# Attention with thresholded softmax and routed experts on one core: value products gathered into every second slot

## The chip, the cores and the metric

The kernel runs on one core of one Trainium2 chip. The metric is device time in microseconds. Three runs of the kernel before gave 980.18 us in the median, 979.74 to 981.54.

## What is computed

Two layers in one launch. Attention over 8 batches, 8 heads, 576 tokens and head size 64, in which every score that lies more than tau below its row's maximum is dropped, and then a mixture of 8 experts in which tokens choose experts greedily under a capacity of 576:

```python
scores = scale * np.matmul(q, k.transpose(0, 1, 3, 2))
thresh = np.max(scores, axis=-1, keepdims=True) - tau
scores = np.where(scores >= thresh, scores, -1000000000.0)
...
attn = np.exp(scores)
attn = attn / (np.sum(attn, axis=-1, keepdims=True) + 1e-09)
return np.matmul(attn, v).astype(np.float32)
...
logits = x @ w_gate          # x: 4608 x 512, then greedy assignment, cap = 576
h = np.maximum(x[mask] @ w1[e], 0.0)
out[mask] = h @ w2[e]        # for each of the 8 experts
```

## The kernel before

Attention takes the first 455 us, the search that assigns tokens to experts starts right behind it, and the experts' matrix products fill the rest. The change touches attention and the stretch in which its last rows are written out; the code of the search and of the experts is the same in both kernels.

**Tiles.** Heads are taken two at a time: 4 head pairs in a batch, 32 in all. Two head pairs (c in the code) make 9 units of queries: four of 128 queries for each pair, and the fifth (u = 4) holds the last 64 queries of both. A unit of two heads is two tiles of 128 queries by 576 keys. A **slot** of the loop handles one unit's two tiles in every stage of the pipeline, so there are 144 slots, and two head pairs take 9 of them.

**Stages of a slot.** TensorE computes the scores (score, line 79) into a tile sc of two PSUM banks, of which the scores fill 288 of 512 columns in each; there are two such tiles, one for each of the slot's two tiles. VectorE takes the row extreme and a scaled copy z (mx, line 87). ScalarE computes the exponentials (ex, line 95) into pp. One slot later VectorE drops what is below the threshold and sums the rows (stt, line 98). Then TensorE transposes pp in blocks of 64 keys (turn, line 108): the first 8 of the 9 key blocks into one PSUM tile tb of which there is one only (tr), which ScalarE copies to pt (trev, line 123). The **ninth** key block of a unit goes into the free columns of a score tile (left), and ScalarE copies it out of there (leftev, lines 136 and 139). The value products of a head pair (group, line 151) run over 9 key blocks, accumulate in the PSUM tile vb, and are copied to xt when the ninth is in (shut, line 155). The trace records each float32 matmul as two, so a key block of products is 8 recorded matmuls; a transpose is recorded once.

**Order.** Each engine runs in the order in which the code issues. In a slot TensorE has: the scores of both tiles, the ninth blocks of one or two units (in 5 of 9 slots), a piece of value products, the 16 transposes of the unit. The dictionary plan gives the pieces: a head pair's 9 key blocks are spread over four slots as 3, 2, 2 and 2; 8 slots of 9 have a piece, and the remaining one has the gate's logits of a finished batch (lg_unit, line 174, or lgt_unit). The transposes' tile is copied out in the next slot. The ninth blocks sit in the score tile of the slot's second tile, and ScalarE copies them out between the two exponentials. For two batches finished rows are transposed into the free columns of score tiles too (rows_turn), at two slots of 9.

**End.** The products of the last two head pairs, the last logits, and then 18 late rows (late_unit, line 218): 8 transposes of 128 by 128 into tb or vb by turns, one copy by ScalarE (line 220), and a copy of 16 factors (line 222) for two units of three; then the rows are written to memory. The first steps of the search (a phase of the Router, whose counting matmuls are at line 453) are issued between the late rows by a small planner, with XTY us from one late row to the next.

Of the kernel before, what the change touches and what calls it, by code (L numbers as in the profile page):

```python
# [18 lines left out]
S=576; D=64; HS=288; QK=2*HS+2*S; NB=9; SL=3; XE=8*HS  # L19
PPB=8; LTB=1; VTB=4; HOLD=1; XW=520; NBO=2; NDEF=4; XTB=4; XTY=1.35; XT0=2.0; XRB=2  # L20


def attention(ctx, tc, qk, vl, tau, wgd, xrows, xts, Lg, nb_batches, ident, swap, R, after_first):
# [101 lines left out]
    def left(s_,t,only=None):  # L125
        c,u=divmod(s_,9)
        if u not in (1,3,6,8) and u!=only or s_<0: return
        sc=SC[t] if t is not None else ps_s.tile([128,2,512],F32,name="sc"); LB[s_]=sc
        for i,n in enumerate((u,) if u==4 else (u-1,u)):
            turn(sc[:,:,HS+64*i:HS+64*i+64],PB.pop((c,n)).rearrange("p k h d -> p k (h d)")[:,8])  # L130
    def leftev(s_):
        c,u=divmod(s_,9)
        if s_ not in LB: return
        sc=LB.pop(s_)
        if u==4:
            for a in range(2): A.activation(pt_of(2*c+a)[:,8].rearrange("p (f q) -> p f q",f=2)[:,:,0:32],sc[:,a,HS:HS+64].rearrange("p (f q) -> p f q",f=2),AF.Copy)
        else:
            p,g=tile_of(c,u); o=at(g-1)
            A.activation(pt_of(p)[:,8,o:o+256].rearrange("p (i r q) -> p r i q",i=2,r=2),sc[:,:,HS:HS+128].rearrange("p r (i q) -> p r i q",i=2),AF.Copy)
# [42 lines left out]
    def lgt_unit(b,ps):  # L182
        lt=LT[b]
        for c in range(5):
            o=at(c) if c<4 else S
            turn(ps[:,:,64*c:64*c+64],lt[:,o:o+128])
    def lv_of(ps): return ps[:,:,:320].rearrange("p r (c j x) -> p r c j x",c=5,j=2)[:,:,:,:,:16]
    def lgt_ev(b,ps):
# [26 lines left out]
    def late_unit(b,qb,k):  # L215
        ps=(ps_v.tile([128,2,512],F32,name="vb") if k%2 else ps_t.tile([128,2,512],F32,name="tb")).rearrange("p a b -> p (a b)")
# [57 lines left out]
    for s_ in range(-2,NT//2+2):  # L274
        st["slot"]=s_
        sc_=[t for t in (2*s_+4,2*s_+5) if 0<=t<NT]; tr_=[t for t in (2*s_,2*s_+1) if 0<=t<NT]
        tt_=[t for t in (2*s_+2,2*s_+3) if 0<=t<NT]; ev_=0<=s_-1<z; gate=None
        for t in sc_: score(t)
        if ev_: left(s_-1,sc_[-1] if sc_ else None)
        if (s_-5)%9==SL: left(s_-1-SL,sc_[-1] if sc_ else None,4)  # L280
        if s_==9: R.consts2()
# [31 lines left out]
        if 0<=s_<z: tr(s_)  # L313
# [648 lines left out]
```

## Time and profile before

| | |
|---|---|
| median of three runs | 980.18 us |
| the profiled execution | 980.79 us, span 979.1 us |
| TensorE matmul busy | 939.3 us, 96% |
| VectorE, ScalarE, GpSimd busy | 761.3, 620.2, 241.3 us |
| chain that ended last | TensorE 83%, ScalarE 6%, VectorE 5%, DMA 2% |
| attention's loop, first to last row extreme of slots 5 to 141 | 25.50 to 435.71 us |
| its last late row copied, search counting ends | 478.8 us, 481.6 us |

Times are from the span's start. The busy column of TensorE contains the modelled tail of each matmul, so a TensorE that is called 99% busy may still wait a little; how densely it works is read from the starts of its instructions. What ended an idle stretch stands behind an arrow.

### The profile page before, as it was taken

Reading aid. Unit: us, or ns where it says so; the run is one execution under the profiler, and the core shown is the slowest. Engines: PE = TensorE matmul, PEld = TensorE weight load, DVE = VectorE, ACT = ScalarE, POOL = GpSimd, SP = SyncE. Lnnn points to the kernel's source line nnn. Section 1 sums busy time; section 2 is a strip of 40 time slices with the busy share of each in tenths; the row PEclk is TensorE's granted clock in tenths of the full one; section 3 lists DMA queues with packets and bytes.
Section 4 is the critical chain, followed back from the end, with each engine's and each line's share of the span. In section 5 each row is a group of like instructions: output and inputs, shape, how many; then the busy total and the mean of one; then the engine's idle time right before and its main releaser. Section 6 shows DMA issues by size and latency. Waiting matters only on the chain.

```text
span 979.1 us, 25952 instructions
## 1 busy us (share of the span) xinstructions
PE 939.3 (96%) x10365; PEld 718.5 (73%) x10365; DVE 761.3 (78%) x2070; ACT 620.2 (63%) x1064; POOL 241.3 (25%) x334
## 2 busy tenths in 40 slices
PE   6999999999999999998789999999999999999996
PEld 4666666666666666665679798897988979898994
DVE  7999999999999999993679878587887786535220
ACT  6889989999899998984445354352452525445330
POOL 2222423333242423220020412222303123210202
PEclk9999999999999999999889999999999999999999
DMA  5213242431523141205651615243523435341101
GB/s 205 87 54 108 72 157 68 156 133 57 183 69 98 44 145 53 99 2 198 235 181 43 217 44 185 66 158 103 164 91 135 125 124 153 120 134 38 38 11 44
DMA packets 38936, 107.63 MB, mean 110 GB/s; under 512 B 7456, under 2 KB 8224, under 8 KB 38304
## 3 DMA queue, kind: packets, MB, share of 16 engines
q1 hardware_dynamic: 31424, 83.36, 25.1%
q0 software_dynamic: 5888, 19.03, 6.3%
q10 hardware_dynamic: 1504, 3.59, 1.2%
q8 instruction: 82, 1.34, 0.6%
q14 instruction: 38, 0.31, 0.1%
HBM read 83.51 MB, written 21.38 MB: 107 GB/s over the span
## 4 chain that ended last, share of the span: by engine, by line
PE 83%; ACT 6%; DVE 5%; issue 2%; DMA 2%; POOL 0%; POOLq 0%; ACTq 0%; SPq 0%; DVEq 0%
PE pf L800 21%; PE pf L832 20%; PE vb L151 13%; PE sc L79 12%; PE tb L108 8%; ACT pp L95 3%; PE pt L745 2%; DVE pp L98 1%; PE sc L108 1%; PE rps L453 1%; DVE z L87 1%; ACT pt L123 1%; ACT pt L120 1%; DMA out_dram<-y,idx 1%; PE vb L174 1%
## 5 line engine op out<-in xcount | busy, mean ns | idle before, releaser
L95 ACT ACTIVATE pp<-z,nb 128x576 f32<-128x576 f32 x288 | 218.4, 777 | 39.9 <-DVE z L87 39.1
L98 DVE SCALAR_TENSOR_TENSOR pp<-z,nb,pp 128x576 f32<-128x576 f32 x288 | 223.8, 814 | 0.0
L87 DVE TENSOR_SCALAR_CACHE_REDUCE z<-sc 128x576 f32<-128x576 f32 x288 | 206.6, 752 | 18.7 <-PE sc L79 11.8
L832 PE MATMUL pf<-w2h,H 128*128 128x512 f32 x576 | 194.3, 401 | 0.2 <-DVE H L381 0.2
L79 PE MATMUL sc<-qk 64*128 64x288 f32 (+1 forms) x1280 | 173.5, 419 | 3.1 <-DMA qk<-qk_dram 1.9
L88 POOL TENSOR_SCALAR nb<-nb,taub 128x2 f32<-128x2 f32 x144 | 99.0, 687 | 284.2 <-ACT pp L95 180.3
L151 PE MATMUL vb<-pt,vt 64*64 64x288 f32 x2232 | 164.9, 416 | 0.3 <-ACT pt L120 0.3
L123 ACT ACTIVATE pt<-tb 128x1024 f32<-128x1024 f32 x128 | 131.0, 1023 | 8.3 <-PE tb L108 7.8
L108 PEld LDWEIGHTS tb<-ident,pp 64*128 64x128 f32 x2304 | 83.5, 139 | 70.9 <-ACT pp L95 36.0
L832 PE MATMUL pf<-w2l,H 128*128 128x512 f32 x320 | 128.6, 402 | 0.0
L839 POOL DMA_INDIRECT out_dram<-y,idx x40 | 45.6, 1140 | 307.5 <-ACT y L835 270.4
L832 PEld LDWEIGHTS pf<-w2h,H 128*128 128x128 f32 x576 | 106.7, 189 | 19.5 <-DVE H L381 0.7
L79 PEld LDWEIGHTS sc<-qk 64*128 64x128 f32 (+1 forms) x1280 | 96.7, 178 | 23.8 <-DVE z L87 4.0
L108 PE MATMUL tb<-ident,pp 64*128 64x64 f32 x2304 | 103.1, 230 | 10.2 <-ACT pt L120 4.3
L151 PEld LDWEIGHTS vb<-pt,vt 64*64 64x64 f32 x2232 | 73.5, 133 | 50.7 <-issue 8.8
L800 PE MATMUL pf<-xh,w1h 128*128 128x288 f32 (+2 forms) x512 | 109.9, 301 | 0.7 <-ACT xh L746 0.7
L800 PE MATMUL pf<-xh,w1l 128*128 128x288 f32 (+2 forms) x512 | 110.4, 301 | 0.0
L800 PE MATMUL pf<-xl,w1h 128*128 128x288 f32 (+2 forms) x512 | 110.1, 301 | 0.0
L835 ACT ACTIVATE y<-pf 128x512 f32<-128x512 f32 x40 | 23.9, 597 | 124.6 <-PE pf L832 115.4
L812 ACT ACTIVATE hf<-pf 128x576 f32<-128x576 f32 x56 | 36.5, 651 | 90.4 <-PE pf L800 85.9
L800 PEld LDWEIGHTS pf<-xh,w1h 128*128 128x128 f32 x512 | 82.1, 190 | 1.6 <-ACT xh L746 1.1
L800 PEld LDWEIGHTS pf<-xl,w1h 128*128 128x128 f32 x512 | 82.0, 190 | 0.0
(189 smaller groups left out, 1202.9 us busy)
## 6 DMA issues: line engine op xcount, KB each, us to landing
qk<-qk_dram SPq DMA_DIRECT2D x31, 864.0 KB, 5.1
w2s<-w_dram SPq DMA_DIRECT2D x32, 512.0 KB, 4.4
w1s<-w_dram SPq DMA_DIRECT2D x28, 512.0 KB, 5.1
vt<-vl_dram SPq DMA_DIRECT2D x32, 288.0 KB, 4.3
xrows<-pp SPq DMA_DIRECT2D x24, 260.0 KB, 2.6
xts<-xt SPq DMA_DIRECT2D x2, 1152.0 KB, 5.2
pt<-xts SPq DMA_DIRECT2D x2, 1152.0 KB, 6.7
xrows<-xr SPq DMA_DIRECT2D x8, 260.0 KB, 2.6
```

What stands on the lines that cost most here:

```text
L79: T.matmul(sc[o,f,:HS], LD[p]["q",h][r,q], LD[p]["k",h][r,:],start=True,stop=True)
L87: V.tensor_scalar(z,SC.pop(t)[:,:,:HS],-0.125,None,op0=ALU.mult,op1=ALU.min,accum_out=nb[:,0,t%2:t%2+1])
L88: G.tensor_scalar(nb[:,1],nb[:,0],taub[:,0:1],None,op0=ALU.add)
L95: A.activation(pview(t),zview(t),AF.Exp,bias=NBI[t][:,0:1],scale=-1.0)
L98: V.scalar_tensor_tensor(pv,zview(t),NBI[t][:,1:2],pv,op0=ALU.is_le,op1=ALU.mult,accum_out=den_of(t//36)[:,n:n+1])
L108: g=slice(64*r,64*r+64); T.transpose(o[:,r],x[g],ident[g,g])
L123: A.activation(pt_of(p)[:,0:8,o:o+128].rearrange("p k (r q) -> p r k q",r=2),tb,AF.Copy)
L151: T.matmul(to[64*f:64*f+64,h,:HS],v[g,64*k:64*k+64],pt[g,k,HS*f:HS*f+HS],start=(k==0),stop=(k==8),skip_group_check=True)
L800: T.matmul(ps[:,h,:n],s[w][:,k,f*128:(f+1)*128],s[x][:,k,cols[h]],start=(i==0),stop=(i==11))
L812: A.activation(hf,ps[:,:,:HS],AF.Relu)
L832: T.matmul(ps[:,0,:],H[:,f,c:c+128],s[w][:,f],start=(f==0 and j==0),stop=e)
L839: G.indirect_dma_start(out=out,out_offset=IOA(ap=s["idx"][:n,t:t+1],axis=0),in_=y[:n],in_offset=None)
```

## The change

- The value products of a head pair stand in two slots instead of four, 4 key blocks and then 5, two slots apart. In a period of 18 slots the even slots but one have products, and the odd ones have none; slot 14 has the gate's logits and slot 15 their transposes.
- A unit's 16 transposes are issued one slot later, right behind the scores, and the products come last in a slot. The copy of the transposes follows in the same slot.
- The ninth blocks are issued between the scores of the slot's two tiles, into the first one's score tile, in 8 slots of 18, of which 7 are slots without value products; two units at a time, or three (with the unit of 64 queries). ScalarE copies them out ahead of the transposes' copy.
- Both exponentials of a slot are issued behind the transposes' copy.
- Rows of finished batches are transposed at three slots of 18 instead of two of 9, all in slots with products.
- At the end the next to last head pair's products are interleaved with the last units' transposes; the last logits' transposes are split, four columns of blocks and then the fifth; a late row is made with 16 transposes of 64 rows instead of 8 of 128, and its copy reads and writes contiguous columns; the planner's distance XTY is 1.25 instead of 1.35.

```diff
-    def mx(ts):
+    def mx(ts,between):
...
             z=wk.tile([128,2,HS],F32,name="z",bufs=5); ZB[t]=z
...
+            if t%2==0: between()
+        if ts: G.tensor_scalar(nb[:,1],nb[:,0],taub[:,0:1],None,op0=ALU.add)
+        else: between()
...
+    NINTH={3:0,7:1,9:2,11:3,13:4,16:5,17:6,1:7}
+    def left(s_,sc):
+        n=NINTH.get(s_%18)
...
+    def leftev():
+        if "now" not in LB: return
+        i0,sc=LB.pop("now"); c,u=divmod(i0,9); p,g=tile_of(c,u); o=at(g)
+        A.activation(pt_of(p)[:,8,o:o+256].rearrange("p (i r q) -> p r i q",i=2,r=2),sc[:,:,HS:HS+128].rearrange("p r (i q) -> p r i q",i=2),AF.Copy)
+        if u==2:
+            for a in range(2): A.activation(pt_of(2*c+a)[:,8].rearrange("p (f q) -> p f q",f=2)[:,:,0:32],sc[:,a,HS+128:HS+192].rearrange("p (f q) -> p f q",f=2),AF.Copy)
...
-        for i in range(8): T.transpose(ps[:n,128*i:128*i+128],xh(b)[:,i,o:o+n],ident)
+        for i in range(8): turn(ps[:n,:,64*i:64*i+64],xh(b)[:,i,o:o+n])
...
-    for p in range(NP-1):
-        n=0; o=9*(p//2)+(10 if p%2 else 6)
-        for i,m in enumerate((3,2,2,2) if p<NP-2 else (3,3,1)): plan[o+i-(p==NP-2)]=[(p,x) for x in range(n,n+m)]; n+=m
+    for p in range(NP-2):
+        o=18*(p//4)+(6,10,16,20)[p%4]
+        plan[o]=[(p,x) for x in range(4)]; plan[o+2]=[(p,x) for x in range(4,9)]
+    plan[z-2]=[(NP-2,x) for x in range(5)]
...
-        for t in sc_: score(t)
-        if ev_: left(s_-1,sc_[-1] if sc_ else None)
+        for t in sc_[:1]: score(t)
+        left(s_,SC[sc_[0]] if sc_ else None)
+        for t in sc_[1:]: score(t)
...
+        if 0<=s_-1<z: tr(s_-1)
...
+        mx(sc_,leftev)
...
+        if 0<=s_-1<z: turned(s_-1)
...
-        for t in sc_[1:]: ex(t)
+        for t in sc_: ex(t); SC.pop(t)
...
-        if 0<=s_<z: tr(s_)
         if s_==z-1:
+            for k in (5,6): group(NP-2,k)
+            tr(z-1); turned(z-1)
             for k in (7,8): group(NP-2,k)
...
-    lgt_unit(b,gp); lgt_ev(b,gp)
+    lgt_unit(b,gp,range(4)); w=lgt_ev(b,gp)
+    gp=ps_s.tile([128,2,512],F32,name="sc")
+    lgt_unit(b,gp,(4,)); lgm_ev(b,gp,w)
```

TensorE in the middle of the loop, before: scores are sc<-qk, ninth blocks sc<-ident,pp, products vb<-pt,vt, transposes tb<-ident,pp.

```order
L79 MATMUL sc<-qk 128x288 x4
L108 MATMUL sc<-ident,pp 128x64 x4
L151 MATMUL vb<-pt,vt 64x288 x8
L108 MATMUL tb<-ident,pp 128x64 x16
L79 MATMUL sc<-qk 128x288 x4
L151 MATMUL vb<-pt,vt 64x288 x12
L108 MATMUL tb<-ident,pp 128x64 x16
```

TensorE in the same place after: a slot without products, one with products, and the next scores.

```order
L79 MATMUL sc<-qk 128x288 x2
L110 MATMUL sc<-ident,pp 128x64 x4
L79 MATMUL sc<-qk 128x288 x2
L110 MATMUL tb<-ident,pp 128x64 x16
L79 MATMUL sc<-qk 128x288 x4
L110 MATMUL tb<-ident,pp 128x64 x16
L156 MATMUL vb<-pt,vt 64x288 x20
```

The product pieces are half as many and about twice as long; between the ninth blocks and the next slot's first scores there are now half a slot's scores and the transposes, where a product piece stood too.

ScalarE in a slot with ninth blocks, before, with the engines that each instruction waits for (pt<-tb is the transposes' copy, pp<-z an exponential, pt<-sc the ninth blocks' copy):

```order
L123 ACTIVATE pt<-tb 128x2x8x64 [waits PE_49]
L95 ACTIVATE pp<-z,nb 128x9x64 [waits DVE_49]
L139 ACTIVATE pt<-sc 128x2x2x64 [waits DVE_49]
L95 ACTIVATE pp<-z,nb 128x9x64
L155 ACTIVATE xt<-vb 128x576 [waits PE_49]
```

ScalarE in such a slot after:

```order
L142 ACTIVATE pt<-sc 128x2x2x64 [waits DVE_49]
L125 ACTIVATE pt<-tb 128x2x8x64 [waits PE_49]
L97 ACTIVATE pp<-z,nb 128x9x64
L97 ACTIVATE pp<-z,nb 128x9x64 [waits DVE_49]
L125 ACTIVATE pt<-tb 128x2x8x64 [waits PE_49]
```

The ninth blocks' copy moved to the head of the slot; it waits for VectorE in both, now for the row extreme of the first tile.

TensorE at the start of the late rows, before (tb<-ident,xt and vb<-ident,xt are late rows, the last row begins the search's first count):

```order
L218 MATMUL tb<-ident,xt 128x128 x8
L218 MATMUL vb<-ident,xt 128x128 x8
L218 MATMUL tb<-ident,xt 32x128 x8
L218 MATMUL vb<-ident,xt 128x128 x8
L218 MATMUL tb<-ident,xt 128x128 x8
L453 LDWEIGHTS cmp
```

And after:

```order
L110 MATMUL tb<-ident,xt 128x64 x16
L110 MATMUL vb<-ident,xt 128x64 x16
L110 MATMUL tb<-ident,xt 32x64 x16
L110 MATMUL vb<-ident,xt 128x64 x16
L464 LDWEIGHTS cmp
```

Four late rows instead of five stand ahead of the first count.

## Rows read from the trace of the kernel before

**Rows 1.** The page's line of busy times by engine, and the view by stretches for 50 us of the loop (busy us and instructions of PE, PEld, DVE, ACT, POOL, then the granted clock of TensorE, the DMA share and GB/s).

```profile
PE 939.3 (96%) x10365; PEld 718.5 (73%) x10365; DVE 761.3 (78%) x2070; ACT 620.2 (63%) x1064; POOL 241.3 (25%) x334
...
250.00:300.00 50.00, 49.55 (x766) 31.57 (x764) 48.81 (x136) 45.15 (x71) 16.17 (x26) 1.00 0.32 112
```

**Rows 2.** The timeline of TensorE for two slots and a bit (start, length with the modelled tail, instruction and count).

```profile
227.76 1.19 PE L79 MATMUL sc<-qk 64*128 64x288 f32 x8
228.78 0.28 PE L108 MATMUL sc<-ident,pp 64*128 64x64 f32 x4
229.00 1.20 PE L151 MATMUL vb<-pt,vt 64*64 64x288 f32 x16
230.13 0.72 PE L108 MATMUL tb<-ident,pp 64*128 64x64 f32 x16
230.68 1.19 PE L79 MATMUL sc<-qk 64*128 64x288 f32 x8
231.80 1.69 PE L151 MATMUL vb<-pt,vt 64*64 64x288 f32 x24
233.42 0.71 PE L108 MATMUL tb<-ident,pp 64*128 64x64 f32 x16
234.06 1.20 PE L79 MATMUL sc<-qk 64*64 64x288 f32 x16
235.19 0.34 PE L108 MATMUL sc<-ident,pp 64*128 64x64 f32 x4
```

**Rows 3.** The timeline of VectorE: the row extreme of the first tile of slots 0, 5, 51, 69, 87, 105 and 141.

```profile
11.33 0.75 DVE L87 TENSOR_SCALAR_CACHE_REDUCE z<-sc 128x576 f32<-128x576 f32 x1
...
25.50 0.75 DVE L87 TENSOR_SCALAR_CACHE_REDUCE z<-sc 128x576 f32<-128x576 f32 x1
...
164.58 0.76 DVE L87 TENSOR_SCALAR_CACHE_REDUCE z<-sc 128x576 f32<-128x576 f32 x1 [0.24 <-PE sc L108]
...
219.81 0.76 DVE L87 TENSOR_SCALAR_CACHE_REDUCE z<-sc 128x576 f32<-128x576 f32 x1 [0.22 <-PE sc L108]
...
273.93 0.75 DVE L87 TENSOR_SCALAR_CACHE_REDUCE z<-sc 128x576 f32<-128x576 f32 x1
...
327.59 0.75 DVE L87 TENSOR_SCALAR_CACHE_REDUCE z<-sc 128x576 f32<-128x576 f32 x1
...
435.71 0.76 DVE L87 TENSOR_SCALAR_CACHE_REDUCE z<-sc 128x576 f32<-128x576 f32 x1 [0.72 <-PE sc L79]
```

**Rows 4.** The timelines of TensorE and ScalarE at places where one engine waited for another: scores and what starts behind them, a copy of ninth blocks (128x256), the pair of small copies of a 64-query unit, two exponentials in a row, and a product that waits for a copy.

```profile
164.26 0.41 PE L108 MATMUL sc<-ident,xt 64*128 64x64 f32 x8
...
230.00 0.38 ACT L139 ACTIVATE pt<-sc 128x256 f32<-128x256 f32 x1
...
232.38 1.45 ACT L95 ACTIVATE pp<-z,nb 128x576 f32<-128x576 f32 x2
...
434.95 1.19 PE L79 MATMUL sc<-qk 64*128 64x288 f32 x8
...
436.51 1.46 ACT L95 ACTIVATE pp<-z,nb 128x576 f32<-128x576 f32 x2 [0.33 <-DVE z L87]
...
441.20 0.34 ACT L136 ACTIVATE pt<-sc 128x64 f32<-128x64 f32 x2
...
445.75 1.02 ACT L123 ACTIVATE pt<-tb 128x1024 f32<-128x1024 f32 x1
...
446.82 4.59 PE L151 MATMUL sc<-pt,vt 64*64 64x288 f32 x70 [0.53 <-ACT pt L123]
```

**Rows 5.** The timeline of TensorE at the end of attention, ahead of the last head pair's products.

```profile
440.07 0.23 PE L108 MATMUL sc<-ident,pp 64*128 64x64 f32 x2
442.07 0.94 PE L108 MATMUL tb<-ident,pp 64*128 64x64 f32 x16 [1.77 <-DVE pp L98]
442.94 2.20 PE L151 MATMUL vb<-pt,vt 64*64 64x288 f32 x16
```

**Rows 6.** The timelines of TensorE and ScalarE in the late rows: the first late row, its copies, and the search's counts 1, 6 and 7 (L453).

```profile
454.76 1.09 PE L218 MATMUL tb<-ident,xt 128*128 128x128 f32 x8
...
455.89 1.02 ACT L220 ACTIVATE pp<-tb 128x1024 f32<-128x1024 f32 x1 [1.99 <-PE tb L218]
...
456.92 1.02 ACT L220 ACTIVATE pp<-vb 128x1024 f32<-128x1024 f32 x1
...
458.06 1.01 ACT L220 ACTIVATE pp<-tb 32x1024 f32<-32x1024 f32 x1
...
459.12 1.02 ACT L220 ACTIVATE pp<-vb 128x1024 f32<-128x1024 f32 x1
...
460.05 0.38 PE L453 MATMUL sc<-oh,cmp 128*128 128x32 bf16 x9
...
478.16 0.39 PE L453 MATMUL rps<-oh,cmp 128*128 128x32 bf16 x9 [0.41 <-DVE cmp L381]
...
481.20 0.42 PE L453 MATMUL rps<-oh,cmp 128*128 128x32 bf16 x9 [1.52 <-DVE cmp L381]
```

**Rows 7.** The view by stretches at the end of attention, in the late rows and behind them (columns as in Rows 1).

```profile
442.30:445.80 3.50, 3.50 (x37) 1.89 (x33) 2.69 (x6) 0.60 (x2) 0.41 (x3) 0.51 0.02 5
...
475.30:479.90 4.60, 3.31 (x43) 2.62 (x40) 2.13 (x7) 3.19 (x5) 0.00 (x0) 1.00 1.01 364
479.90:490.20 10.30, 6.30 (x82) 5.62 (x83) 7.65 (x27) 1.06 (x1) 0.00 (x0) 0.50 0.46 158
```

More of the change, by code (lines that the diff above doesn't have):

```diff
@@ L124, in attention, with ninth @@
     LB={}
[L125 to L139, printed above, removed]
+    NINTH={3:0,7:1,9:2,11:3,13:4,16:5,17:6,1:7}
+    def left(s_,sc):
+        n=NINTH.get(s_%18)
+        if n is None: return
+        i0=18*(s_//18-(n==7))+9*(n//4)+(0,2,5,7)[n%4]
+        if not 0<=i0<NT//2: return
+        if sc is None: sc=ps_s.tile([128,2,512],F32,name="sc")
+        ninth(i0,sc)
+    def ninth(i0,sc):
+        LB["now"]=(i0,sc)
+        for i in range(3 if i0%9==2 else 2):
+            turn(sc[:,:,HS+64*i:HS+64*i+64],PB.pop(divmod(i0+i,9)).rearrange("p k h d -> p k (h d)")[:,8])
+    def leftev():
[4 more added lines that the diff above has]
+            for a in range(2): A.activation(pt_of(2*c+a)[:,8].rearrange("p (f q) -> p f q",f=2)[:,:,0:32],sc[:,a,HS+128:HS+192].rearrange("p (f q) -> p f q",f=2),AF.Copy)
     XT={}
@@ L181, in ltev, with lgt_unit @@
         for k in range(2): G.tensor_scalar(lt[:,S+64*k:S+64*k+64].rearrange("p (f q) -> p f q",f=2)[:,f],m[:,f,0:32],1.0,0.0,op0=ALU.mult,op1=ALU.add)
-    def lgt_unit(b,ps):
+    def lgt_unit(b,ps,cs=range(5)):
         lt=LT[b]
-        for c in range(5):
+        for c in cs:
             o=at(c) if c<4 else S
@@ L194, in lgt_ev, with lgm_ev @@
         V.tensor_reduce(Lg[:,4*b:4*b+4,:],w[:,0:4].rearrange("p c r j h e -> p c e (r j h)"),axis=AX.X,op=ALU.add)
+        return w
+    def lgm_ev(b,ps,w):
+        lv=lv_of(ps).rearrange("p r c j (h e) -> p r c j h e",h=2)
         g=slice(64*(b%2),64*(b%2)+64)
@@ L311, in attention @@
         columns()
-        if s_==z-2: R.prep(0,28); R.compare(R.k("E1"),J,0,28)
-        if 0<=s_<z: tr(s_)
+        if gate and not gate[1]:
+            for h in range(2):
+                for f in range(2): lg_unit(gate[0],f,vb,(h,))
+            pend.append(lambda b=gate[0]: ltev(b,(0,1),vb))
         if s_==z-1:
+            for k in (5,6): group(NP-2,k)
+            tr(z-1); turned(z-1)
             for k in (7,8): group(NP-2,k)
             pend.append(lambda: shut(NP-2))
+            R.prep(0,28); R.compare(R.k("E1"),J,0,28)
+            break
     p=NP-1; b=p//4
+    ninth(z-2,ps_s.tile([128,2,512],F32,name="sc")); leftev()
+    for g in soon: g()
     flush()
-    for g in soon: g()
     gp=ps_s.tile([128,2,512],F32,name="sc")
@@ L337, in attention @@
     R.ps=lambda: ps_s.tile([128,2,512],F32,name="sc")[:,0]
-    ph=R.phase(); now=nxt=0.0; at=XT0
+    ph=R.phase(); now=nxt=at=0.0; R.V.free=XT0; first=True
     while late:
@@ L342, in attention @@
         else:
-            now=at; late.pop(0)(); at=now+XTY
+            now=at; late.pop(0)(); at=now+(XTY if not first else 0.6); first=False
     return ph,(nxt if nxt<1e6 else 0.0)
```

44 lines of the change are left out of this document (16 added, 28 removed).

## Prediction

> **What bounds the kernel now.** I read the page's busy times first and then the stretch of 50 us in the loop [rows 1]: TensorE is busy for 49.55 us of 50, VectorE for 48.81, ScalarE for 45.15, at a granted clock of 1.00. Three engines close to full mean that a saving on one is worth only what the next one leaves. The timeline of TensorE [rows 2] shows its pieces start to start with no gap between them: scores 1.02 us ahead of ninth blocks and 1.12 ahead of products, ninth blocks 0.22, products of 2 key blocks 1.13 and of 3 key blocks 1.62, transposes 0.55 ahead of scores and 0.64 ahead of a piece of another shape. The timeline of VectorE [rows 3] gives the length of slots: 273.93 to 327.59 is 18 slots in 53.66 us, 2.98 each; 164.58 to 219.81 is 18 slots with four transposed pieces of finished rows, 55.23, so such a piece costs 0.39; slots 5 to 141 take 410.21. In the first slots, where no products are made, five take 14.17 us (11.33 to 25.50), so VectorE's own floor is 2.83 a slot. TensorE bounds the loop and VectorE stands 5% behind it.
>
> **The change, part by part.** The sum is made on the profiled execution, 980.79 us, of which 1.7 us lie outside the span; the median of the three runs is 0.61 lower, and I carry the difference over to the median.
>
> TensorE's own work: 3 key blocks against 2 are 0.49 us more, so a product piece is 0.15 plus 0.49 per key block, 2.11 for 4 and 2.60 for 5 [rows 2]. Eight pieces less in 18 slots are 8 x 0.15 = 1.2 us. Entering a piece costs 0.10 (1.12 against 1.02) or 0.09 (0.64 against 0.55), eight times less often, 0.8. Ninth blocks between two scores make one more seam, at most 0.06 each, 8 x 0.06 = 0.5 back. The net is 1.5 us in 18 slots, 53.66 to 52.2. If that were all, the loop would win 7.56 x 1.5 = 11 us.
>
> It is not all, since the even slots are now long and the odd ones short, and the odd ones have lost the product piece that covered the ninth blocks' way out. In an odd slot with ninth blocks this chain runs. The first tile's scores take 0.51 (half of 1.02), and the row extreme waits for the ninth blocks in the same tile: where four transposes stood behind scores before, it began 0.32 after the first of them (164.26 to 164.58) [rows 3, 4], so 0.83. The copy of the ninth blocks is queued for VectorE's row extreme, and ScalarE starts 0.80 after that begins (435.71 to 436.51). The copy takes 0.38. TensorE starts 0.05 after a copy's end (446.77 to 446.82) [rows 4]. Only then can the next slot's first scores go into this tile. That is 2.06 us from score to score, in which TensorE has only its scores, ninth blocks and transposes, 1.02 + 0.22 + 0.55 = 1.79: it waits 0.27 us. The even slot adds 1.02 + 0.64 + 2.11 = 3.77, or 4.26 with 5 key blocks. So a pair of slots takes 5.83 or 6.32 us, against VectorE's 5.67.
>
> The eighteen slots, from odd row extreme to odd row extreme: 17 to 1, 6.32; 1 to 3, 5.83; 3 to 5, 6.25 (no ninth blocks in slot 5, the extreme 0.76 behind the scores, 434.95 to 435.71); 5 to 7, VectorE's 5.67; 7 to 9, 6.62 (three units, the copies 0.3 longer, bounded by the 0.34 of such a pair [rows 4]); 9 to 11, 5.83; 11 to 13, 6.32; 13 to 15 and 15 to 17 with the logits, 5.67 each. Two slots have scores of the other shape, 1.13 instead of 1.02 [rows 2], 0.22 together. Sum 54.40, against 53.66. Slots 5 to 141 are then 30.2 for the first ten and 7 x 54.40, 411.0. The 12 pieces of finished rows cost 4.7 before; in slot 6 VectorE covers them now, so 8 x 0.39 = 3.1. The loop is 414.1, **3.9 us longer**.
>
> Bounds of this term: if the row extreme did not wait for the ninth blocks (0.76 in place of 0.83), 6 times in 18 slots, it is 0.4 x 7.56 = 3 us less. If the copy comes late in ScalarE's queue, each 0.1 us in seven odd slots costs 7 x 7.56 x 0.1 = 5.3 us. I take 0.83, since the row is a row extreme behind just such transposes.
>
> What else is moved in the loop costs nothing. The transposes, a slot later, find their unit finished a slot earlier; the eight pp buffers just hold a unit from its exponential to its ninth block, seven slots later. Both exponentials behind the transposes' copy are ready when ScalarE comes to them, and the masks that wait for them are a slot away. GpSimd's threshold and the loads on the sync queue stand where they stood. The cover of ScalarE is thin, see the second rival.
>
> End of attention: from the last slot's row extreme to the last head pair's products it took 435.71 to 446.82, 11.11 us, with 1.77 of idling for VectorE and then a piece of 2 key blocks at 2.20 in place of 1.13, at a granted clock of 0.51 [rows 5, 7]. After: 0.85 until the score tile is free, ninth blocks of three units 0.3, transposes 0.64, 5 key blocks 2.60, ninth blocks 0.22, transposes 0.64, 2 key blocks 1.13, transposes 0.64, 1.13, ninth blocks 0.22: 8.4, without a gap long enough for the clock to fall as it did. **Minus 2.7.** Bounds: minus 1.5 if two waits for transposes' copies show, minus 3.2 if the extreme is not awaited.
>
> Late rows: the search's first count came 5.29 us after the first late row began (454.76 to 460.05), behind five rows [rows 6]. Now four rows stand ahead. A late row's transposes end 0.72 after their start instead of 1.09 [rows 2, 6], but ScalarE's copies follow each other every 1.03 to 1.14, and the fourth row needs the second copy's end: 0.77 + 1.03 + 1.02 + 0.05 = 2.87, plus 0.55 and a seam, 3.5. That is 1.8 earlier. From count 1 to count 6 took 18.11, five steps of 3.62. A step runs through VectorE and through one or two late rows; ScalarE still paces the rows, so I give each step 0.12, and 0.6 in all. The last step, 3.04, has no late rows. **Minus 2.4**; bounds 0, if the copies pace everything, and minus 4, if eleven rows on the chain each save 0.37. The rows' writes fill the DMA engines in the last of this (share 1.01 in 475.30 to 479.90 [rows 7]); the gather that reads them comes after the search, which covers them; without that cover the gain would be lost.
>
> One stretch of this hangs on the clock. While little but late rows and counts ran on TensorE, its granted clock was 1.00, the 2.4 GHz level, still in 475.30 to 479.90, and it fell to 0.50, 1.2 GHz, only when they had ended [rows 7]. The Trainium skill (TensorE: Matmul & The Clock Gate, Part 4: PE-mode transpose) says that transposes do not count as busy for the clock. By that rule the late rows should have run at 1.2 GHz already, which the trace does not bear out; by the rule the gain here would be about 0, by the row 2.4. Half as much streaming per late row is nevertheless a reason to doubt, and it is the third rival.
>
> Sum: +3.9 - 2.7 - 2.4 = **-1.2**, 979.6 us in the profiled execution, 979.0 in the median: too little to tell. About 0.2%, 2 us, is what a measurement of this kernel can tell from no change.
>
> **The rivals.** First, the odd slots' chain is hidden and TensorE is bound by its own 52.2 us in 18 slots: 410.2 - 11 + 3.1 - 4.7, and with the end and the late rows 980.2 - 12.6 - 5.1 = 962.5. For it: the pieces of rows 2 add up to that, and VectorE's 51.0 allows it. Against it: the copy's wait stands in the order, and TensorE has nothing to do in the 0.27.
>
> Second, on the other side: ScalarE is late for the ninth blocks. In a pair of slots it has two copies of 1.02, four exponentials at 0.67 to 0.78 (two in 1.45 [rows 4]), a ninth copy and half a copy of products, some 5.6 of 5.83. Nothing happens while the exponentials of an even slot end before the next odd row extreme plus 0.80; from there every 0.1 costs 5.3 us. At 0.15 late: 979.0 + 8 = 987.
>
> Third, the clock falls in the late rows: a row's transposes took 0.94 at 0.51 against 0.72 [rows 2, 5], so their saving is gone, and the 2.4 with it: 981.4, and up to 2 us more if the counts slow down too.
>
> Fourth, what the end wins is given back behind the search, where weights are loaded and rows gathered: without 2.7 and 2.4 it is 984; with one half back, 981.5.
>
> **How the numbers follow.** The forecast's own spread: 0.05 us in the chain of seven odd slots is 2.6 us, the end and the late rows 1.5 each, so 979.0 give or take 3.5. Forecast 0.54 (of it 0.22 below 978.2, 0.26 within, 0.06 above 982.1), first rival 0.12, second 0.15, third 0.12 (half of it above 982.1), fourth 0.07 (0.04 within, 0.03 above). Faster 0.34, within 0.36, slower 0.30. The range leaves out the first rival and half of the second: 971 to 986.
>
> **What would show it.** In the profile after: 18 slots in the middle of the loop at 54.4 us by row extremes; TensorE idle 0.2 to 0.3 in odd slots, released by ScalarE's ninth copy; VectorE idle about 0.6 ahead of odd row extremes behind 5 key blocks, released by TensorE. Product pieces of 2.11 and 2.60. From the last row extreme to the last head pair's products 8.4. The first count 3.5 after the first late row, and counts 1 to 6 in 17.5. I am wrong if 18 slots take under 53 or over 55.5, if the late rows show a clock of 0.5, or if the experts' stretch differs by over 1.5 us.

## The result and the profile after

The changed kernel takes 988.56 us in the median of four runs (986.28 to 989.90), against 980.20 for the kernel before on the same chip: a ratio of 1.0081, with a 95% interval of 1.0059 to 1.0102. It is slower by 8.4 us, where 979.0 was forecast and 986 was the end of the range. The profiled execution took 989.90 us, with a span of 988.0.

The page after: busy times, the chain that ended last by engine, and the row extremes (L87) and scores (L79) with their idle time and what ended most of it.

```profile
PE 937.1 (95%) x10509; PEld 732.5 (74%) x10509; DVE 760.3 (77%) x2065; ACT 614.5 (62%) x1066; POOL 245.6 (25%) x340
...
PE 80%; ACT 7%; issue 5%; DVE 3%; DMA 2%; POOL 1%; ACTq 0%; POOLq 0%; DVEq 0%; SPq 0%
...
L87 DVE TENSOR_SCALAR_CACHE_REDUCE z<-sc 128x576 f32<-128x576 f32 x288 | 206.3, 752 | 29.1 <-PE sc L110 20.2
...
L79 PE MATMUL sc<-qk 64*128 64x288 f32 (+1 forms) x1280 | 196.1, 441 | 19.4 <-ACT pt L142 10.3
```

The same two groups on the page before:

```profile
L87 DVE TENSOR_SCALAR_CACHE_REDUCE z<-sc 128x576 f32<-128x576 f32 x288 | 206.6, 752 | 18.7 <-PE sc L79 11.8
...
L79 PE MATMUL sc<-qk 64*128 64x288 f32 (+1 forms) x1280 | 173.5, 419 | 3.1 <-DMA qk<-qk_dram 1.9
```

The time is not in more work: TensorE's matmuls, VectorE and ScalarE are busy 2.2, 1.0 and 5.7 us less than before, and only GpSimd, at a quarter of the span, is busy 4.3 us more. The time is in waits. TensorE stood idle for 19.4 us ahead of scores (3.1 before), more than half of it for ScalarE's copy of the ninth blocks (L142), and VectorE 29.1 us ahead of row extremes (18.7 before), most of it for the ninth blocks' transposes (L110).

The stretch of 50 us in the loop shows the same (columns as in [rows 1]):

```profile
300.00:350.00 50.00, 47.77 (x730) 32.63 (x734) 47.03 (x132) 43.33 (x70) 15.97 (x28) 1.00 0.28 95
```

TensorE, VectorE and ScalarE are each 1.8 us less busy in 50 us than in [rows 1], at the same clock: now none of the three is full.

The row extremes of the first tile of slots 5, 15, 51, 69, 105, 123 and 141, which answer to [rows 3]:

```profile
26.04 0.75 DVE L87 TENSOR_SCALAR_CACHE_REDUCE z<-sc 128x576 f32<-128x576 f32 x1
...
56.48 0.75 DVE L87 TENSOR_SCALAR_CACHE_REDUCE z<-sc 128x576 f32<-128x576 f32 x1
...
167.96 0.75 DVE L87 TENSOR_SCALAR_CACHE_REDUCE z<-sc 128x576 f32<-128x576 f32 x1
...
224.01 0.75 DVE L87 TENSOR_SCALAR_CACHE_REDUCE z<-sc 128x576 f32<-128x576 f32 x1
...
335.74 0.75 DVE L87 TENSOR_SCALAR_CACHE_REDUCE z<-sc 128x576 f32<-128x576 f32 x1
...
391.19 0.75 DVE L87 TENSOR_SCALAR_CACHE_REDUCE z<-sc 128x576 f32<-128x576 f32 x1
...
446.64 0.75 DVE L87 TENSOR_SCALAR_CACHE_REDUCE z<-sc 128x576 f32<-128x576 f32 x1
```

Slots 5 to 141 take 420.60 us, against 410.21 before. Eighteen slots without finished rows take 55.45 (335.74 to 391.19), with them 56.05.

TensorE from slot 15 to the scores of slot 18, which answers to [rows 2]:

```profile
335.17 0.66 PE L110 MATMUL tb<-ident,pp 64*128 64x64 f32 x16
336.38 0.82 PE L110 MATMUL vb<-ident,lt 64*128 64x64 f32 x10 [0.55 <-ACT lt L185]
337.04 0.75 PE L79 MATMUL sc<-qk 64*128 64x288 f32 x4
337.59 0.38 PE L110 MATMUL sc<-ident,pp 64*128 64x64 f32 x6
337.77 0.74 PE L79 MATMUL sc<-qk 64*128 64x288 f32 x4
338.31 0.69 PE L110 MATMUL tb<-ident,pp 64*128 64x64 f32 x16
338.93 2.17 PE L156 MATMUL vb<-pt,vt 64*64 64x288 f32 x32
341.03 0.76 PE L79 MATMUL sc<-qk 64*128 64x288 f32 x4
341.62 0.28 PE L110 MATMUL sc<-ident,pp 64*128 64x64 f32 x4
341.74 0.71 PE L79 MATMUL sc<-qk 64*128 64x288 f32 x4
342.28 0.66 PE L110 MATMUL tb<-ident,pp 64*128 64x64 f32 x16
343.18 1.24 PE L79 MATMUL sc<-qk 64*128 64x288 f32 x8 [0.24 <-ACT pt L142]
```

ScalarE in the same stretch, the logits' copy (L185) and then an odd slot's ninth blocks (L142), and VectorE's row extreme that the ninth blocks wait for:

```profile
334.33 1.45 ACT L97 ACTIVATE pp<-z,nb 128x576 f32<-128x576 f32 x2
335.67 0.66 ACT L185 ACTIVATE lt<-vb 128x576 f32<-128x576 f32 x1
...
342.75 0.38 ACT L142 ACTIVATE pt<-sc 128x256 f32<-128x256 f32 x1 [0.52 <-DVE z L87]
...
341.95 0.76 DVE L87 TENSOR_SCALAR_CACHE_REDUCE z<-sc 128x576 f32<-128x576 f32 x1 [0.37 <-PE sc L110]
```

Two waits are to be seen. In slot 17 the chain runs as forecast: scores at 341.03, row extreme 0.92 later at 341.95, the copy 0.80 behind that at 342.75, the next scores at 343.18. TensorE had finished its own work and waited 0.24; in the whole trace scores waited 38 times for this copy, 10.3 us in all, 0.27 each. The other one was not in the forecast: the logits' transposes (vb<-ident,lt) stand ahead of the next scores on TensorE and wait for ScalarE's copy, which is queued behind two exponentials, and the last two of them for GpSimd's two small copies behind it. Slot 16's scores begin at 337.04. The row of ten logits' transposes took 0.66 to the next start, where such a row took 0.41 in the profile before (438.36 to 438.77): without 0.55 for ScalarE and 0.25 for GpSimd TensorE would have come to these scores at 336.2.

The end of attention and the late rows (L156 sc<-pt,vt are the last head pair's products, L464 the counts; the first row stands for [rows 5], the others for [rows 6]):

```profile
455.43 4.59 PE L156 MATMUL sc<-pt,vt 64*64 64x288 f32 x72
...
463.32 0.67 PE L110 MATMUL tb<-ident,xt 64*128 64x64 f32 x16
...
466.78 0.39 PE L464 MATMUL sc<-oh,cmp 128*128 128x32 bf16 x9
...
470.20 0.39 PE L464 MATMUL sc<-oh,cmp 128*128 128x32 bf16 x9 [0.45 <-DVE cmp L392]
474.42 0.39 PE L464 MATMUL sc<-oh,cmp 128*128 128x32 bf16 x9
...
484.57 0.41 PE L464 MATMUL rps<-oh,cmp 128*128 128x32 bf16 x9 [0.97 <-DVE cmp L392]
487.72 0.43 PE L464 MATMUL rps<-oh,cmp 128*128 128x32 bf16 x9 [1.52 <-DVE cmp L392]
```

The view by stretches, for the late rows between counts 2 and 3 and for the start of the experts' products (506.09):

```profile
471.00:474.40 3.40, 3.36 (x53) 2.85 (x52) 2.05 (x9) 2.20 (x4) 0.00 (x0) 0.50 0.98 348
...
506.10:515.30 9.20, 9.07 (x41) 8.56 (x42) 8.30 (x24) 3.42 (x11) 0.00 (x0) 0.50 0.69 238
```

At a clock of 0.50, the 1.2 GHz level, a step that takes 3.4 us elsewhere took 4.22 (470.20 to 474.42), and the experts began with 9.2 us at this level.

The two profiles side by side, stretch by stretch (us, from starts of instructions):

| stretch | before | after | measured | forecast |
|---|---|---|---|---|
| start to slot 5's row extreme | 25.50 | 26.04 | +0.5 | 0 |
| slots 5 to 141 | 410.21 | 420.60 | +10.4 | +3.9 |
| to the last head pair's products | 11.11 | 8.79 | -2.3 | -2.7 |
| to the first late row | 7.94 | 7.89 | 0.0 | 0 |
| to count 7 | 26.44 | 24.40 | -2.0 | -2.4 |
| to the first expert product | 18.80 | 18.37 | -0.4 | 0 |
| to the end of the span | 479.1 | 481.9 | +2.8 | 0 |
| sum | | | +8.9 | -1.2 |

The first row is not the change's: this stretch took 25.3 to 26.5 us in the other profiles, whichever kernel ran. The last head pair's products are counted from their unbroken row (446.82 before, [rows 4]; 455.43 after).

### The profile page after: what moved, and what is told of

It is laid out like the page before. It is cut to its first block, busy times and chain, and to the rows that moved or that the text cites. A ratio compares the mean times of both kernels' runs of the same rounds, so it can differ in the third digit from the quotient of the medians.

```text
span 988.0 us, 26085 instructions
## 1 busy us (share of the span) xinstructions
PE 937.1 (95%) x10509; PEld 732.5 (74%) x10509; DVE 760.3 (77%) x2065; ACT 614.5 (62%) x1066; POOL 245.6 (25%) x340
## 4 chain that ended last, share of the span: by engine, by line
PE 80%; ACT 7%; issue 5%; DVE 3%; DMA 2%; POOL 1%; ACTq 0%; POOLq 0%; DVEq 0%; SPq 0%
PE pf L811 22%; PE pf L843 20%; PE vb L156 14%; PE sc L79 12%; PE tb L110 5%; ACT pp L97 2%; PE pt L756 2%; ACT pt L142 2%; PE sc L110 1%; DVE z L87 1%; ACT pt L125 1%; PE rps L464 1%; DMA out_dram<-y,idx 1%; ACT pt L122 1%; PE vb L110 1%
## 5 line engine op out<-in xcount | busy, mean ns | idle before, releaser
L87 DVE TENSOR_SCALAR_CACHE_REDUCE z<-sc 128x576 f32<-128x576 f32 x288 | 206.3, 752 | 29.1 <-PE sc L110 20.2
L79 PE MATMUL sc<-qk 64*128 64x288 f32 (+1 forms) x1280 | 196.1, 441 | 19.4 <-ACT pt L142 10.3
L97 ACT ACTIVATE pp<-z,nb 128x576 f32<-128x576 f32 x288 | 208.1, 779 | 6.5 <-DVE z L87 6.5
L156 PE MATMUL vb<-pt,vt 64*64 64x288 f32 x2232 | 149.9, 408 | 0.0
L79 PEld LDWEIGHTS sc<-qk 64*128 64x128 f32 (+1 forms) x1280 | 93.9, 180 | 71.1 <-DVE z L87 16.5
L110 PEld LDWEIGHTS tb<-ident,pp 64*128 64x128 f32 x2304 | 93.0, 139 | 25.2 <-ACT pt L125 4.6
L156 PEld LDWEIGHTS vb<-pt,vt 64*64 64x64 f32 x2232 | 79.2, 133 | 42.9
L110 PE MATMUL tb<-ident,pp 64*128 64x64 f32 x2304 | 97.1, 224 | 0.0
L811 PEld LDWEIGHTS pf<-xh,w1l 128*128 128x128 f32 x512 | 82.5, 191 | 0.2
```

Source lines behind the costliest of these rows:

```text
L79: T.matmul(sc[o,f,:HS], LD[p]["q",h][r,q], LD[p]["k",h][r,:],start=True,stop=True)
L87: V.tensor_scalar(z,SC[t][:,:,:HS],-0.125,None,op0=ALU.mult,op1=ALU.min,accum_out=nb[:,0,t%2:t%2+1])
L97: A.activation(pview(t),zview(t),AF.Exp,bias=NBI[t][:,0:1],scale=-1.0)
L110: g=slice(64*r,64*r+64); T.transpose(o[:,r],x[g],ident[g,g])
L156: T.matmul(to[64*f:64*f+64,h,:HS],v[g,64*k:64*k+64],pt[g,k,HS*f:HS*f+HS],start=(k==0),stop=(k==8),skip_group_check=True)
L811: T.matmul(ps[:,h,:n],s[w][:,k,f*128:(f+1)*128],s[x][:,k,cols[h]],start=(i==0),stop=(i==11))
```

## The experiments

For the loop two theories stand against each other: the waits in odd slots (the ninth blocks' copy) and in slot 15 (the logits), or the alternation of long and short slots itself, with ScalarE late. For the experts' 2.8 us it is the level of the clock against a delay of loads or gathers. The kernels ran on four chips, on which the kernel before took 984.8, 981.6, 991.0 and 980.6 us, so ratios are compared, and traces stretch by stretch.

**The late rows alone, on the kernel before.** The functions and the loop at the end of attention were taken over, and nothing of the slots:

```diff
-        for i in range(8): T.transpose(ps[:n,128*i:128*i+128],xh(b)[:,i,o:o+n],ident)
+        for i in range(8): turn(ps[:n,:,64*i:64*i+64],xh(b)[:,i,o:o+n])
...
-            now=at; late.pop(0)(); at=now+XTY
+            now=at; late.pop(0)(); at=now+(XTY if not first else 0.6); first=False
```

> The kernel before with the late rows of the change alone: 16 transposes of 64 rows, contiguous copies, four rows ahead of the first count, distance 1.25, the last logits' transposes split; the loop and the end of the loop are those of before. Theory (the late rows gain what the two traces show, 26.44 to 24.40 us from the first late row to count 7): 980.2 - 2.0 = 978.2, first late row to count 7 about 24.4. Rival (the gain is given back behind the search or to a lower clock in the late rows, as the clock of 0.5 for 3.4 us in the late rows of after suggests): 980 to 981, with a stretch at 0.5 in the late rows.

Measured: ratio 0.9988 (0.9974 to 1.0002), 1.2 us below before's median, which the interval does not tell from zero. The trace has the first late row to count 7 in 24.26 us (26.44 before), the first count 3.46 behind the first late row, and a stretch at 0.5 in them, in which one step took 4.06. So the late rows gain 2.2 us even with a fall of the clock; in the total it isn't settled, since its end of attention had 6.8 us at 0.5 and its experts' stretch began with 9.6 us at 0.5.

**The ninth blocks moved to slots with products.** Each of these eight slots gets one copy, and the finished rows had to go elsewhere, since they use the same columns (two lines that match the units to the new slots are not printed here):

```diff
-    NINTH={3:0,7:1,9:2,11:3,13:4,16:5,17:6,1:7}
+    NINTH={4:0,6:1,8:2,10:3,12:4,16:5,0:6,2:7}
...
-        rt=bool(rows) and sc_ and s_%18 in (2,6,10)
+        rt=bool(rows) and sc_ and s_%18 in (1,5,9)
```

> The changed kernel with the ninth blocks moved to the eight slots with products (slots 4, 6, 8, 10, 12, 16, 0, 2 of 18), and the pieces of finished rows to slots 1, 5, 9. Theory (the loop is long because in odd slots the next scores wait for the ninth blocks' copy with nothing on TensorE to cover it): a pair behind 5 key blocks takes 0.80 + 4.26 + 0.22 + 0.76 = 6.04 us, the others VectorE's 5.67 but for the logits' 6.21, so 18 slots fall from 55.45 to about 53.3 and the time from 988.6 to about 972. Rival (long and short slots by turns are the cost themselves, and the exponentials behind the transposes' copy make ScalarE late): 18 slots stay at 55 or more, 987 to 995.

Measured: slower, ratio 1.0121 (1.0096 to 1.0147). By the time alone this is the rival's result; the trace says otherwise. Eighteen slots without rows take 53.35 us, as expected (341.40 to 394.75), and eighteen with rows 58.36:

```profile
167.85 0.75 DVE L87 TENSOR_SCALAR_CACHE_REDUCE z<-sc 128x576 f32<-128x576 f32 x1
...
226.21 0.75 DVE L87 TENSOR_SCALAR_CACHE_REDUCE z<-sc 128x576 f32<-128x576 f32 x1
...
341.40 0.75 DVE L87 TENSOR_SCALAR_CACHE_REDUCE z<-sc 128x576 f32<-128x576 f32 x1
...
394.75 0.75 DVE L87 TENSOR_SCALAR_CACHE_REDUCE z<-sc 128x576 f32<-128x576 f32 x1
```

On the page the wait for L142 no longer leads ahead of the scores, and another copy has its place (xr are the finished rows):

```profile
L79 PE MATMUL sc<-qk 64*128 64x288 f32 (+1 forms) x1280 | 195.2, 439 | 24.9 <-ACT xr L269 17.1
```

The rows had been put into odd slots, where each of 12 pieces now made TensorE wait 1.4 us for a copy that stands behind the transposes' copy, at 1.67 us a piece ((58.36 - 53.35) / 3). It looks like the theory's own mechanism, moved to another tenant of the score tile, which I had not priced; whether it is, the run after the next two shows.

**The logits at the end of slot 13.**

```diff
-        gate=aux.pop(0) if aux and (s_%18==14 and not aux[0][1] or s_%18==15) else None
+        gate=aux.pop(0) if aux and (s_%18==13 and not aux[0][1] or s_%18==15) else None
```

> The changed kernel with the logits at the end of slot 13 in place of 14; their transposes stay in slot 15. Theory (slot 15 costs 0.54 us over the forecast because the logits' transposes wait for ScalarE's copy, which is queued behind slot 14's exponentials, and for GpSimd behind it): 15 to 17 falls from 6.21 to about 5.7, 7 times 0.5 = 3.5 us less, 985. Rival (the 0.54 is VectorE's or the alternation's, and the wait only stands where another would): 988 to 989.

Measured: ratio 1.0058 (1.0038 to 1.0079), against the changed kernel's 1.0081. The two intervals overlap, so the trace has to decide. From slot 15 to 17 takes 5.76 us (334.68 to 340.44), 0.45 less, while 13 to 15 grew from 5.68 to 5.78; eighteen slots take 55.09. Slots 5 to 141 take 418.59, 2.0 less. In the trace the logits' transposes no longer wait:

```profile
333.89 0.71 PE L110 MATMUL tb<-ident,pp 64*128 64x64 f32 x16
334.44 0.47 PE L110 MATMUL vb<-ident,lt 64*128 64x64 f32 x10
335.49 0.76 PE L79 MATMUL sc<-qk 64*128 64x288 f32 x4 [0.57 <-DVE z L87]
```

What ends TensorE's idle time there is now VectorE, whose slots 15 and 16 take 2.84 and 2.92, close to its own pace of 2.83 [rows 3]. The wait is shown, at somewhat more than half of its expected price in the loop. The changed kernel has a control of its own: in its first period, in which no batch is finished and slot 15 has no logits, 15 to 17 takes 5.73, and 6.20 to 6.21 in all six others.

**Both moves.** The two edits above together.

> Both: ninth blocks in the slots with products and the logits at the end of slot 13. Theory: the two gains add up, 972 - 3.5 = 968.5, 18 slots 52.8. Rival (VectorE's 51.0 or ScalarE takes over, so that the second gain is hidden): as with the ninth blocks alone.

Measured: 1.0088 (1.0060 to 1.0117); eighteen slots without rows 53.12 (expected 52.8), with rows again 58 to 59.7, the longest with 3.4 us at a clock of 0.5 in it. Where no rows are, the logits' move gains another 0.23 on top of the ninth blocks', half of what was expected, and the rows cost more than both gain.

**Rows in slots with products too,** in the columns that two units' ninth blocks leave free (of a piece's four blocks one in the first tile and three in the second). The edit is shown against the kernel with the ninth blocks moved; the line with the copy's new columns is not printed here:

```diff
-        rt=bool(rows) and sc_ and s_%18 in (1,5,9)
+        rt=bool(rows) and sc_ and s_%18 in (2,8,10)
...
-            o=XN["sc"][i//2]; e=HS+64*(i%2)
+            o=XN["sc"][i>0]; e=HS+(64*(i-1) if i else 128)
```

> The changed kernel with the ninth blocks in the eight slots with products, and the pieces of finished rows in three of these too (2, 8, 10 of 18), in the columns that the ninth blocks leave free. Theory (any piece in a score tile's free columns whose copy ScalarE makes in a slot without products holds up the next scores; the run with ninth blocks moved lost its gain because each of 12 pieces of rows in an odd slot cost 1.65 us): 18 slots with rows fall from 58.4 to about 54.3, without rows stay at 53.35; slots 5 to 141 about 407, 15 less than there, and with the end and late rows of the change a ratio to before near 0.992. Rival (rows cost the same wherever they stand, by their transposes and ScalarE's copies): 18 slots with rows stay at 57 or more, the ratio above 1.00.

Measured: **faster than both kernels**, ratio 0.9904 (0.9890 to 0.9918), 971.89 us against 981.57. Slots 5 to 141 take 405.69; eighteen slots take 54.2 with rows and 53.34 without (324.47 to 377.81), so a piece of rows costs 0.29 here and 1.67 in an odd slot. On its page:

```profile
L87 DVE TENSOR_SCALAR_CACHE_REDUCE z<-sc 128x576 f32<-128x576 f32 x288 | 205.5, 749 | 15.9 <-PE sc L79 14.8
...
L79 PE MATMUL sc<-qk 64*128 64x288 f32 (+1 forms) x1280 | 195.6, 441 | 7.8 <-DVE z L87 4.7
```

The product pieces of 4 and 5 key blocks are the same, and so are the exponentials behind the transposes' copy: only the tenants of the score tiles' free columns have moved, and TensorE's idle time ahead of scores fell from 19.4 to 7.8 us, VectorE's ahead of row extremes from 29.1 to 15.9. The rival of the alternation falls with this, and the rows' price in the odd slots is shown to be one of place.

**The same with the logits at the end of slot 13.**

> The same with the logits at the end of slot 13. Theory: 18 slots without rows 53.1, slots 5 to 141 about 405, ratio 0.990. Rival (VectorE is the bound, the logits' wait is hidden): as without it.

Measured: 0.9912 (0.9897 to 0.9927). Slots 5 to 141 take 404.28, 1.4 less than without it, and eighteen slots 53.11, as expected; but the time is not better. In its profile the clock fell to 0.5 a little ahead of count 3 and stayed there beyond the end of the late rows:

```profile
457.30:481.10 23.80, 17.45 (x258) 14.77 (x255) 13.44 (x42) 10.39 (x17) 0.00 (x0) 0.50 0.68 238
```

The first late row to count 7 took 26.09 us there, against 23.47 in the run before it, whose late rows are the same and ran at 1.00.

**Both kernels again,** for the stretches that the change leaves alone.

> The changed kernel again, for the stretches that the code doesn't touch. If the 2.8 us by which the experts' products took longer come from where the clock's level changes fall, this profile has the same loop (420.6) and another length of the experts' stretch, by half the time that TensorE was at 0.5 in it. If the change itself slows the experts (loads or gathers that arrive later), the stretch is longer than before's by about 2.8 again, at the same level of the clock.

> The kernel before again, for its stretches on this chip: loop 410.2, first late row to count 7 26.4, experts' stretch as in the profile before but for the time that TensorE is at 0.5.

Measured: the changed kernel 1.0083 (1.0068 to 1.0097), loop 420.52; before again, one run of 979.76, loop 410.20, late rows 26.44. The end of attention differs between the two profiles of the kernel before. In the first the clock had fallen there [rows 7]; in this one it had not, and the last head pair's products began 9.89 us behind the last row extreme (436.18) and not 11.11:

```profile
442.30:445.80 3.50, 2.74 (x38) 1.51 (x38) 3.13 (x9) 1.35 (x2) 0.46 (x2) 1.00 0.02 5
...
446.07 4.59 PE L151 MATMUL sc<-pt,vt 64*64 64x288 f32 x70 [0.79 <-ACT pt L123]
```

So at equal levels the new end gains 1.1 us (8.79 against 9.89), and the other 1.2 of the table's 2.3 belong to a fall of the level in one profile of before.

The start of the experts, in the changed kernel and in the one before:

```profile
506.50:515.70 9.20, 9.07 (x41) 8.56 (x42) 8.29 (x24) 3.37 (x11) 0.00 (x0) 0.50 0.65 236
```

```profile
499.00:502.60 3.60, 3.60 (x17) 3.60 (x18) 3.48 (x12) 2.43 (x9) 0.00 (x0) 0.50 0.62 169
```

On this one chip the experts' stretch took 479.07 us with 3.6 us at 0.5 at its start (before again), 480.01 with 4.2 (rows and ninth blocks moved), 481.52 with 9.2 (after again) and 481.90 with 9.6 (logits moved too). The theory had expected another length in the second profile of the changed kernel, and it came out the same, so the repetition alone decides nothing. Where the time goes does. TensorE was 99% busy in the 9.2 us, so it was not waiting for loads, and the same 32 products into the stretch are reached 9.94 us behind the first one (506.09) after and 7.80 (500.00) before. Shown are the product reached after, the same one before, and a product of after that waits much later in the stretch:

```profile
516.03 0.75 PE L811 MATMUL pf<-xh,w1l 128*128 128x320 f32 x4
...
507.80 0.75 PE L800 MATMUL pf<-xh,w1l 128*128 128x320 f32 x4
...
609.83 0.73 PE L843 MATMUL pf<-w2h,H 128*128 128x512 f32 x2 [0.42 <-DVE H L392]
```

All fourteen profiles fall into two groups here: 7.8 to 7.9 us where the level stayed at 0.5 for 3.1 to 4.6 us, and 9.9 to 10.3 where it did for 9.2 to 9.6. So 2.1 of the 2.8 us go with the level. The rival is right in a smaller part: the wait of 0.42 at 609.83 stands in all twelve profiles with the changed late rows, that of the late rows alone among them, and in neither of the kernel before; its cause was not followed. The last 0.3 are not placed. Nor is the level all that makes two runs differ: on another chip two kernels with the same start (ninth blocks moved, and both moves) had experts' stretches of 483.28 and 486.15. No run set the level by itself.

**Idle matmuls behind the search's steps,** 12 of them behind each of seven, on three of the kernels:

```diff
                 held(0.1); E=s.step_n(E)
+                if s.alone: s.warm(12)
```

> The changed kernel with 12 idle matmuls of 128 by 128 bf16 behind each of the search's first seven steps, where TensorE waits some 1.5 us for VectorE. Theory (the changed late rows leave TensorE so little to do that its clock falls in them, and the next fall behind the search then lasts until 9.3 us into the experts' products instead of 3.8): the clock stays at 1.00 through the late rows, first late row to count 7 takes 23.5 in place of 24.4, and the experts' products start at a higher level, 481.9 minus up to 4.6 us; 988.6 becomes 984 to 987. Rival (the fillers delay late rows and counts by as much, 0.6 each, or the level falls all the same behind the search): 988 to 992.

> The kernel with ninth blocks and rows in the slots with products, and the same fillers. In its profile the late rows were at 1.00 and the experts began with 4.2 us at 0.5. Theory: at most half of that is won, 2 us, ratio to before 0.988 to 0.990. Rival (the fillers only delay): 0.991 to 0.995.

> The same with the logits at the end of slot 13, whose late rows ran at 0.5 for 23.9 us in the profile taken (26.09 from the first late row to count 7, against 23.47 at 1.00) and whose times spread from 970.4 to 975.9. Theory (its spread is the clock's): with fillers the late rows take 23.5, and the time is 968 to 970 with a spread below 2 us, ratio 0.987. Rival (the fillers don't hold the level, or delay): 972 to 975 as before.

Measured: 1.0059 (1.0036 to 1.0082), 0.9911 (0.9890 to 0.9931) and 0.9899 (0.9875 to 0.9923). The times that the theories expected did not come (984 to 987 us for the first, 0.988 to 0.990 and 0.987 for the others). All three profiles kept 1.00 through the late rows, and counts 1 to 5 followed each other every 3.41 to 3.43 us. But count 6 to 7 took 3.72 instead of 3.03, and count 7 to the first expert product 19.8 to 20.2 instead of 18.4 to 18.8. In the changed kernel:

```profile
483.95 0.39 PE L464 MATMUL rps<-oh,cmp 128*128 128x32 bf16 x9 [0.27 <-DVE cmp L392]
...
487.68 0.39 PE L464 MATMUL rps<-oh,cmp 128*128 128x32 bf16 x9 [1.52 <-DVE cmp L392]
```

The level still fell behind the search, and the experts of the changed kernel began at 0.5 all the same. Two of these kernels had lost the level in the late rows in all three profiles without fillers, so the fillers seem to hold it there; behind the last steps, where nothing else runs, they delayed what follows by 0.7 and by 1.3 to 1.5.

**Idle matmuls behind the first five steps only,** on the kernel with all three moves (ninth blocks, rows, logits):

> Ninth blocks and rows in the slots with products, logits at the end of slot 13, and idle matmuls behind the first five steps of the search only, those beside which late rows run. Theory (the fillers hold the level in the late rows; behind the last two steps they delayed the next count by 0.7 and what follows by 1.3): first late row to count 7 takes 23.5 at a clock of 1.00, count 7 to the first expert product 18.7, and the ratio to before is 2 us below the run with all fillers, 0.988. Rival (without the last two fillers the level falls sooner and the counts slow down): 0.990 or more, late rows to count 7 over 24.5.

Measured: 0.9900 (0.9883 to 0.9916), 971.33 us against 980.58. The late rows take 23.46 at 1.00, count 6 to 7 again 3.04 and count 7 to the experts 18.57, as the theory has it in the trace. The time does not follow: 0.988 was expected, and 0.990 is within the intervals of the versions without fillers. The best ratio here, 0.990, is shared by all the versions with ninth blocks and rows in the slots with products, which can't be told apart.

## Why the prediction was wrong, point by point

**The odd slots' chain was right and too short.** The forecast had 2.06 us from score to score; slot 17 shows 2.15 (341.03 to 343.18), since the row extreme began 0.92 and not 0.83 behind the scores: half of a slot's scores, followed by ninth blocks, took 0.59 to the next start (341.03 to 341.62), where half of 1.02 had been set. Of the nine pairs, read from the row extremes of slots 103 to 121, seven came within 0.2 of their forecast (6.41 for 6.32, 6.29 for 6.25, 6.63 for 6.62, 6.51 for 6.32, 5.87 for 5.83, 6.03 for 5.83, 5.83 for 5.67 behind three units' ninth blocks), and 13 to 15 was 5.68 for 5.67. Together these are 0.5 us in 18 slots over the forecast, after the 0.22 that was set aside for the other shape, and 3.6 in the loop. This is a mis-sized term: the text itself said that 0.1 in seven odd slots costs 5.3.

**The step that failed** is "13 to 15 and 15 to 17 with the logits, 5.67 each". 15 to 17 took 6.21. I let VectorE's floor stand for it, and did not follow the logits' transposes through ScalarE's queue: the copy that they need is issued behind two exponentials, and the product piece that stood on TensorE meanwhile is gone. At 0.54 in the six periods with logits, and 0.06 in the one without, it is 3.3 in the loop, and moving the logits took 0.45 of it away from that pair. With the 12 pieces of rows at 2.5 instead of 3.1 (their slots are partly covered) and 0.2 in the first ten slots, the loop is 6.5 above the forecast.

**Why the chain is there.** The ninth blocks' copy by ScalarE and the row extreme by VectorE read the same bank, and the copy began only when the extreme had read it: 0.80 behind its start (341.95 and 342.75), and 0.79 or 0.80 in all 61 copies of the loop. The wait is in the program, as the order of ScalarE's instructions shows. The Trainium skill (PSUM — Partial Sum Buffer, Terms) says that two engines must not access one bank of the same partitions at once, reads against reads included; the trace agrees in that no copy of ninth blocks ran beside the first tile's extreme here. A version with the ninth blocks in a bank of their own was not tried.

**The end and the late rows** were forecast at -5.1 and gave -4.3, in part by luck. The end measured 8.79 for 8.4; the logits' transposes waited 0.55 there too, but with the logits moved it was still 8.69, with waits for VectorE and ScalarE in their place. The forecast named the fall of the clock in the 11.11 of before and took it for a fixed part of that kernel; against the profile without the fall the end gains 1.1 and not 2.7. The late rows measured 24.40 for 24.0; where the clock held and no fillers ran, they took 23.47 to 23.58, a gain of 2.9 to 3.0.

**The third rival came true in part.** The clock fell in the late rows of four of the eight profiles that have the changed late rows and no fillers, in neither profile of before, and in none of four with fillers. It costs 0.8 to 0.9 when the fall lasts 3.4 us and 2.6 when it lasts through. The Trainium skill (TensorE: Matmul & The Clock Gate, Part 4: PE-mode transpose), by which the full clock does not engage for transposes, since they don't count as busy in the same way, is not borne out as it stands: by it the level would have fallen in all of these without fillers, and it held at 1.00 in six of ten, the two of before among them. Why it falls in one run and not in another of the same late rows stays open.

**The experts' stretch** was named as a reason to be wrong (over 1.5 us), but had no term and no chance of its own. The level had fallen 4.4 us ahead of the first expert product in after and 3.0 in before, and TensorE spent 9.2 and 3.8 us of the products at 0.5: that is 2.1 of the 2.8 measured, by the first 32 products. It is the fourth rival, then, mostly by another mechanism than the one named: the level, and with 0.4 a wait that came with the late rows.

**The first rival** (odd slots' chain hidden, 52.2 in 18 slots) was not reached by any version: with the free columns' tenants in covered slots and the logits moved it is 53.11. The second (ScalarE late, 987) gives nearly the measured time, but not by its mechanism: the copy in slot 17 waited for VectorE with 0.52 us of idle time on ScalarE, and so did 60 of the 64 copies, 48.3 us in all.

## What to carry to other kernels

Before pieces of work are gathered into fewer slots, list for every slot that loses its piece which copies were made under its cover, all tenants of the shared tile among them (here ninth blocks, finished rows and logits), and put these where the long pieces go; the same change was 0.8% slower or 1.0% faster by this alone. When an experiment for a theory comes out the wrong way, look at the stretches that its side edit didn't touch before dropping the theory. A gain of a few microseconds around a stretch with little TensorE work can be lost or doubled by where the clock's level falls (the end's 1.1 showed as 2.3), so stretches are compared at equal levels, and a baseline's stretch is profiled twice before a term is built on it.

## What the runs showed that was not expected

The start of the experts' products at 0.5 lasted 3.1 to 4.6 us in eight profiles and 9.2 to 9.6 in six, with nothing between, and came out the same in both profiles of one kernel (3.8 and 3.6 before, 9.2 and 9.2 after). It is worth 2.1 us, and the code of this stretch is the same in all of them; what decides between the two was not tested. The kernel before took 980 to 991 us on different chips. The loop doesn't take part in that: in the profiles it was 410.2 in three profiles of before's loop and 420.5 to 420.6 in three of after's, wherever they ran, while the experts' stretch was 479 to 482 us on the quicker chips and 483 to 489 on the others.
